# Attention feeding a two-layer MLP on one core: sums moved behind the landing of what they read, one pair turned on TensorE, and a wrapped batch turned in two DMA pieces

## The chip, the core and the metric

The kernel runs on one core of a Trainium2 chip. The metric is the device time of one execution in microseconds (us); lower is better. Time before: 416.68 us, the median of three runs (415.06, 416.68, 417.58).

## What is computed

```python
# q, k, v: (8, 12, 448, 64) f32;  moe_w_in: (768, 2048);  moe_w_out: (2048, 768)
scores = np.matmul(q, k.transpose(0, 1, 3, 2)) / np.sqrt(64)
attn = softmax(scores)                            # over the last axis
x = np.matmul(attn, v).transpose(0, 2, 1, 3).reshape(3584, 768)
h = x @ w_in
out = np.maximum(0.01 * h, h) @ w_out             # (3584, 768) f32
```

## The kernel before

**Units of work.** The heads of a batch are taken in twos: `NU` = 48 pairs, six (`HP`) to a batch. A pair is loaded from HBM by DMAs that GpSimd issues, cast to bf16 (`cast`, L168 and L170, mostly on GpSimd), and its q and k are turned so that the head's width lies on the partitions. Pairs below `NPE` = 14 are turned on TensorE (`transposes`, L253, copied out of PSUM by VectorE at L259), the others by a transposing DMA from SyncE's queue (`turn`, L236). A pair's scores are four chunks. Three chunks at a time are a **burst**: six matmuls (L270) into three PSUM slots, then three exponentials on ScalarE (L279). When a pair's four chunks are exponentiated, its **rows** follow: 32 matmuls of `e` with `v` (L750) into a slot, a reciprocal and a multiplication on VectorE (L756, L757) that write `x` and free the slot. Then `x` is turned into `xT`, the MLP's input with the model dimension on partitions: by a DMA on SyncE's queue, or for the pairs in `X_PE` (10 and 11 before) on TensorE (L318, copied by L319).

**The MLP** is done by regions of tokens, whose borders are `cuts` = 0, 640, 1152, 1664, 2176, 2688, 3072, 3584. Region 0 is done plainly: `head` takes its first 448 tokens (L352, ScalarE's activation L593), `neck` the other 192 (L616, activation L633, and `mix_h`, L430 and L431). Every later region is a two by two block product in seven products in place of eight, which needs sums of blocks: of w_in (`mix_w_in`, L385 and L389), of w_out (`mix_weights`, L364 to L371), of x (`mix_x_part`, L410) and of h. `hidden(i)` is the first layer of region i (L458), `second(i)` the second layer of region i (`block_pair`, L530; evicted and joined by VectorE at L535 and L538). In `second(i)` the rows of region i + 1 are finished, and its x sums are made there too, since `hidden(i + 1)` comes next.

**xT is a ring** of `NX` = 1920 tokens, with region 3 (token 1664) at place 0. Batch 3 (tokens 1344 to 1791) runs past the ring's end. Its rows are cut in chunks of 112 tokens, one of which straddles the end, 96 columns before it and 16 behind.

**Order.** All five engines run their instructions in the order in which the code emits them. Attention work is put between the matmuls of `head`, `neck` and `second` by `place`, a planner with a rough clock (`model`): it emits a burst, a turning on TensorE or a pair's rows when its model says that slots and inputs are free. SyncE's queue holds the transposing DMAs and the stores of the output in one order.

Of the kernel before, what the change touches and what calls it, by code (L numbers as in the profile page):

```python
# [10 lines left out]
BF16 = mybir.dt.bfloat16  # L11
# [5 lines left out]
def kernel(  # L17
# [9 lines left out]
    nc = tc.nc  # L27
# [3 lines left out]
    P = 128  # L31
# [63 lines left out]
    def place_of(t):  # L95
        return (t + NX - cuts[3]) % NX

    xT = xT_pool.tile([P, KD, NX], BF16)

    w_in_sb = w_pool.tile([P, KD, DF], BF16)  # L100
    w_out_sb = w_pool.tile([P, MD, DM], BF16)
# [133 lines left out]
    def turn(dst, src):  # L235
        nc.sync.dma_start_transpose(out=dst.rearrange("p (c s) -> p c s", s=SC), in_=src)  # L236
# [64 lines left out]
    def x_transposes(u, bank=None):  # L301
        b, hp = divmod(u, HP)
        at = place_of(b * S)
        if bank is None:
            x = x_t.pop(u).rearrange("p so h d -> p so (h d)")
            if at + S <= NX:
                turn(xT[:, hp, at:at + S], x.rearrange("p so n -> p (so n)"))
                return
            fit, rest = divmod(NX - at, SC)
            turn(xT[:, hp, at:at + fit * SC], x[:, :fit].rearrange("p so n -> p (so n)"))  # L310
            nc.sync.dma_start_transpose(out=xT[:, hp, NX - rest:], in_=x[:rest, fit])
            nc.sync.dma_start_transpose(out=xT[:, hp, :SC - rest], in_=x[rest:, fit])
            turn(xT[:, hp, SC - rest:at + S - NX], x[:, fit + 1:].rearrange("p so n -> p (so n)"))
            return
        dst = xT[:, hp, at:at + S]
        tr = turn_tile(bank)
        for so in range(NSC):
            nc.tensor.transpose(tr[:, 0, ts(so, SC)], x_t[u][:, so], ident[:SC, :SC])  # L318
        nc.vector.tensor_copy(dst, tr[:, 0, :])  # L319
# [37 lines left out]
    def mix_weights():  # L357

        pieces = [(slice(m, m + 2), slice(MH + m, MH + m + 2)) for m in range(0, MH, 2)]
        left, right = slice(0, NW), slice(NW, DM)  # L360
        for todo in (pieces[:2], pieces[2:]):
            for lo, hi in todo:
                t2, t3, t4 = (w_mix[:, x, lo] for x in range(3))
                nc.vector.tensor_sub(t3, w_out_sb[:, hi, right], w_out_sb[:, lo, right])  # L364
                yield
                nc.vector.tensor_add(t2, t3, w_out_sb[:, lo, left])
                yield
                nc.vector.tensor_sub(t4, w_out_sb[:, hi, left], t2)
                yield
            for lo, hi in todo:  # L370
                nc.vector.tensor_sub(w_out_sb[:, lo, right], w_out_sb[:, lo, right], w_out_sb[:, lo, left])  # L371
                yield

    def mix_w_in():
# [22 lines left out]
    def mix_x_part(i, ks):  # L397

        at = place_of(cuts[i])
        nh = (cuts[i + 1] - cuts[i]) // 2  # L400
        near, far = slice(ks.start, ks.stop), slice(KH + ks.start, KH + ks.stop)
        one, two = slice(at, at + nh), slice(at + nh, at + 2 * nh)
        t2, t3, t4 = (x_mix[:, x, near, :nh] for x in range(3))
        for o, x, y in (
            (t3, xT[:, far, two], xT[:, near, two]),
            (xT[:, near, two], xT[:, near, two], xT[:, near, one]),
            (t2, xT[:, far, two], xT[:, near, two]),
            (t4, xT[:, far, one], t2),
        ):
            nc.vector.tensor_sub(o, x, y)  # L410
            yield
# [172 lines left out]
    def head(ins, outs):  # L584

        for m in opened:
            part(0, m, (KD - 1,))
        for m in range(MD):
            if m not in opened:
                part(0, m, range(KH))  # L590
                yield KH * HEAD / 2400, False
                part(0, m, range(KH, KD))
            nc.scalar.activation(h[:, m, :HEAD], open_t.pop(m)[:, :HEAD], AX.Prelu, alpha=0.01)  # L593
            settle()
            if m == opened[-1]:
                slots.append(idle)
            if 5 <= m < 13:
                next(ins)
            if m >= 12:
                next(outs)  # L600
            yield (KH if m not in opened else 1) * HEAD / 2400, True

    def neck(outs):

        n = cuts[1] - HEAD
        at = place_of(HEAD)
        ms = [x + y for x in range(0, MH, 2) for y in (0, MH)]
        held = {}

        def part2(m, kks):  # L610
            fresh = m not in held
            if fresh:
                held[m] = next_bank()
            for j in range(2):
                for kk in kks:
                    nc.tensor.matmul(  # L616
                        held[m][:, j * n:(j + 1) * n], w_in_sb[:, kk, ts(m + j, P)], xT[:, kk, at:at + n],
                        start=(fresh and j == 0 and kk == 0), stop=(kk == KD - 1), skip_group_check=True,
                    )

        for m in ms[:2]:
            part2(m, range(KD - 1))
        yield 4 * (KD - 1) * n / 2400, False
        for x, m in enumerate(ms):
            if x < 2:
                assert rows_done >= need[1], rows_done
                settle_x()
                part2(m, (KD - 1,))
            else:
                part2(m, range(KH))  # L630
                yield 2 * KH * n / 2400, False
                part2(m, range(KH, KD))
            nc.scalar.activation(  # L633
                h[:, m:m + 2, HEAD:cuts[1]], held.pop(m)[:, :2 * n].rearrange("p (m t) -> p m t", m=2), AX.Prelu, alpha=0.01
            )
            settle()
            if m >= MH:
                mix_h(0, m - MH)
            for _ in range((1, 1, 1, 1, 0, 2, 2, 2)[x]):
                next(outs)  # L640
            yield 2 * (KH if x > 1 else 1) * n / 2400, True

# [136 lines left out]
            late.extend(todo[2:])  # L779
        chunk += len(todo)  # L780

    X_PE = (HP + 4, HP + 5)
    owed_x = []

    def settle_x(now=None):
# [42 lines left out]
    def place(i, want, soon=0, full=True, calm=True, first=False, lazy=False, keen=NU):  # L828
# [3 lines left out]
        while True:  # L832
# [14 lines left out]
            if want > done and state < 2 and turned(last) and not blocked and len(slots) == 3 and all(  # L847
# [13 lines left out]
                        ready[(start + x) // NSC] = model["act"] + 0.1  # L861
                model["now"] = now + 0.78
                continue
            u = rows_done
            if calm and whole and not (lazy and late) and at[0] <= now + 0.05 and ready.get(u, 0) <= now + 0.05 and (
                u <= (chunk + 5) // NSC - NE or u < keen
# [10 lines left out]
    def second(i):  # L877

        x_sums = [mix_x_part(i + 1, slice(0, 2)), mix_x_part(i + 1, slice(2, 3))] if i + 1 < NR else []
        fresh = [0, 0]  # L880
        left = plan[i]
        for c in range(len(spots(i)[1])):
            for x, _ in enumerate(block_pair(i, c)):
# [3 lines left out]
                    model["now"] += 0.65  # L887
                left -= place(i, left, calm=x not in (1, 3), keen=need[min(i + 2, NR)])
                if i == 0 and x % 2:
                    next(outs if c == 0 and x in (3, 5) else ins if x > 4 else iter(()), None)  # L890
                for y in range(2):
                    fresh[y] += i + 1 < NR and rows_done >= need[i + 2] - 1 + y and 14 * c + x > 4
                for y, todo in enumerate(x_sums):
                    if fresh[y] > 4 and next(todo, 0) is None:
                        break
        assert left == 0 or chunk == NU * NSC, (i, left)
        assert i + 1 == NR or rows_done >= need[i + 2], (i, rows_done)
# [62 lines left out]
```

## Time and profile before

| | |
|---|---|
| median of three runs | 416.68 us |
| the profiled execution | 413.6 us |
| its span | 411.8 us |
| TensorE busy | 385.3 us, 94% of the span |
| VectorE, ScalarE, GpSimd busy | 229.5, 264.8, 142.2 us |
| mean granted TensorE clock | 0.979 of full speed |

The profiled execution is 1.8 us longer than its span (launch and end lie outside), and 3.1 us below the median. A row of the timeline gives the start, the time to the end of the last of its instructions, the engine, the line, the operation, and in brackets how long the engine sat idle before it and what ended that. Matmuls overlap a little in the records, so the time from one row's start to the next row's start is the cost of a row.

### The profile page before, as it was taken

To read this page: it belongs to the slowest core of one execution; us is meant where nothing else is said; L and a number is where in the kernel's file an instruction comes from. 1 tells how busy PE (TensorE), PEld (TensorE's weight loads), DVE (VectorE), ACT (ScalarE), POOL (GpSimd) and SP (SyncE) were. 2 spreads that over 40 slices of the span, in tenths; PEclk is the share of its full clock that TensorE was granted. 3 is DMA by queue.
4 is the path that set the end of the run, shared out by engine and by line. 5 is a ranking of instruction groups with operands and counts; after the bars stand their busy time and mean duration, and the time that the engine had idled before them with its cause. 6 is when DMAs were issued, how large, how long until landed. Compare 5 with 4: busy or idle time off the path is not lost.

```text
span 411.8 us, 9991 instructions
## 1 busy us (share of the span) xinstructions
PE 385.3 (94%) x4074; PEld 263.2 (64%) x4074; DVE 229.5 (56%) x486; ACT 264.8 (64%) x391; POOL 142.2 (35%) x222
## 2 busy tenths in 40 slices
PE   8999976779979999599999999999999999999996
PEld 3564645555648855278655886558855597568854
DVE  3652543476665654354736656465665657384754
ACT  6987861565656877518777588774877668727800
POOL 8898722464346212334043620337112200000000
PEclk9999998699999999979999999999999999999999
DMA  9999999647978913759439891599818650222022
GB/s 137 198 202 203 177 176 194 86 65 113 181 110 141 161 33 61 154 100 170 69 84 152 132 169 26 105 153 167 112 24 149 87 123 2 60 63 78 2 66 88
DMA packets 95038, 47.09 MB, mean 114 GB/s; under 512 B 53648, under 2 KB 91664, under 8 KB 94992
## 3 DMA queue, kind: packets, MB, share of 16 engines
q0 software_dynamic: 38224, 22.58, 43.3%
q1 hardware_dynamic: 56704, 23.85, 28.9%
q8 instruction: 32, 0.52, 0.5%
q14 instruction: 14, 0.11, 0.1%
q10 hardware_dynamic: 64, 0.02, 0.0%
HBM read 45.61 MB, written 11.01 MB: 137 GB/s over the span
## 4 chain that ended last, share of the span: by engine, by line
PE 79%; DMA 8%; DVE 5%; SPq 3%; issue 2%; ACT 1%; POOL 1%; DVEq 0%; ACTq 0%; POOLq 0%
PE g L530 27%; PE g L458 13%; PE sc L458 13%; PE sc L750 9%; PE sc L270 7%; DMA xT<-x 6%; PE g L352 3%; PE g L616 2%; DMA w_in_mix<-in_k_dram 2%; PE g L289 2%; SPq L236 2%; PE g L253 1%; POOL w_in_mix L139 1%; DVE x L757 1%; DVE o L535 1%
## 5 line engine op out<-in xcount | busy, mean ns | idle before, releaser
L279 ACT ACTIVATE e<-sc 112x896 bf16<-112x896 f32 x192 | 163.1, 918 | 48.6 <-PE sc L270 48.3
L530 PEld LDWEIGHTS <-h 128*128 128x128 bf16 x680 | 62.0, 98 | 55.6 <-issue 22.4
L530 PE MATMUL g<-w_out_sb,h 128*128 128x384 bf16 x448 | 86.6, 330 | 7.3 <-DVE o L535 7.3
L168 POOL COPY qkb<-fq 112x512 bf16<-112x512 bf16 x38 | 26.9, 708 | 94.4 <-DMA qkT<-qkb 60.5
L447 ACT ACTIVATE h<-c 128x512 bf16<-128x512 f32 (+1 forms) x72 | 43.5, 611 | 24.0 <-DVE c L473 15.4
L458 PEld LDWEIGHTS <-w_in_sb 128*128 128x128 bf16 x576 | 54.7, 98 | 6.6 <-issue 0.7
L270 PE MATMUL sc<-qkT 64*128 64x448 bf16 x384 | 50.7, 356 | 7.3 <-DVE x L757 4.7
L750 PEld LDWEIGHTS <-e 112*128 112x128 bf16 x1344 | 48.1, 99 | 8.8 <-ACT e L279 6.5
L170 POOL COPY v<-fv 112x512 bf16<-112x512 bf16 x38 | 25.9, 684 | 74.7 <-PE sc L750 70.6
L750 PE MATMUL sc<-v,e 112*128 112x65 bf16 x1344 | 51.5, 196 | 0.0
L458 PEld LDWEIGHTS <-w_in_mix 128*128 128x128 bf16 x432 | 41.2, 98 | 4.1
L530 PE MATMUL g<-w_mix,h 128*128 128x384 bf16 (+1 forms) x224 | 41.9, 327 | 0.0
L270 PEld LDWEIGHTS <-qkT 64*128 64x128 bf16 x384 | 15.0, 94 | 34.6 <-issue 24.6
L535 DVE COPY o<-g 128x384 f32<-128x384 f32 x53 | 29.2, 552 | 13.0 <-PE g L530 12.5
L756 DVE RECIPROCAL rec<-sc 112x8 f32<-112x8 f32 x42 | 8.7, 207 | 44.2 <-PE sc L750 39.8
L168 POOL COPY qkb<-fk 112x512 bf16<-112x512 bf16 x38 | 24.6, 648 | 16.3 <-DMA fk<-in_k_dram 16.3
L757 DVE TENSOR_TENSOR x<-sc,rec 112x512 bf16<-112x512 f32 x42 | 29.0, 691 | 1.6 <-DVE rec L756 0.2
L538 DVE TENSOR_TENSOR o<-o,g 128x384 f32<-128x384 f32 x42 | 23.1, 550 | 10.7 <-PE g L530 10.7
L458 PE MATMUL g<-xT,w_in_sb 128*128 128x256 bf16 (+1 forms) x216 | 28.5, 268 | 0.3 <-DVE o L538 0.3
L458 PE MATMUL sc<-xT,w_in_sb 128*128 128x256 bf16 (+1 forms) x216 | 28.5, 268 | 0.0
L470 ACT COPY c<-g 128x512 f32<-128x512 f32 (+1 forms) x12 | 6.8, 569 | 31.6 <-PE g L458 26.6
L530 PE MATMUL g<-w_mix,hmix 128*128 128x384 bf16 x112 | 21.5, 327 | 0.0
(96 smaller groups left out, 471.8 us busy)
## 6 DMA issues: line engine op xcount, KB each, us to landing
fq<-in_q_dram POOLq DMA_DIRECT2D x19, 224.0 KB, 7.6
fk<-in_k_dram POOLq DMA_DIRECT2D x19, 224.0 KB, 9.1
fv<-in_v_dram POOLq DMA_DIRECT2D x19, 224.0 KB, 6.6
w_in_sb<-in_moe_w_in_dram POOLq DMA_DIRECT2D x4, 768.0 KB, 11.9
w_out_sb<-in_moe_w_out_dram POOLq DMA_DIRECT2D x4, 768.0 KB, 17.5
out_dram<-o SPq DMA_DIRECT2D x7, 336.0 KB, 3.5
out_dram<-o SPq DMA_DIRECT2D x8, 288.0 KB, 4.8
out_dram<-o SPq DMA_DIRECT2D x7, 240.0 KB, 3.1
```

The costliest lines, as they stand in the source:

```text
L168: by(qk_sb[u][:, x].rearrange("p so h d -> p h so d"), f)
L170: by(v_sb[u % NV][:, :, :, :D], f)
L270: nc.tensor.matmul(ps[:, j, :S], t[j * D:(j + 1) * D, S + c * SC:S + c * SC + P], t[j * D:(j + 1) * D, :S], start=True, stop=True,)
L279: nc.scalar.activation(e[:, :, c, :], sc_t.pop((u, c))[:SC, :, :S], AX.Exp, scale=scale)
L352: nc.tensor.matmul(open_t[m][:, :n], w_in_sb[:, kk, ts(m, P)], xT[:, kk, at:at + n], start=(fresh and kk == kks[0]), stop=(kk == KD - 1),)
L447: nc.scalar.activation(hs[:, m:m + 2, cols], x.rearrange("p (m t) -> p m t", m=2), AX.Prelu, alpha=0.01)
L458: nc.tensor.matmul(ps[:, j * nh:(j + 1) * nh], w[:, kk, ts(j, P)], x[:, kk], start=(first and j == 0 and kk == 0), stop=(kk == KH - 1), sk ...
L530: nc.tensor.matmul(ps[:, cols], x[:, m], w[:, m], start=(first and m == 0), stop=(m == MH - 1), skip_group_check=True,)
L535: by(o[:, at], ps[:, :NW])
L538: nc.vector.tensor_add(o[:, at], o[:, at], ps[:, :NW])
L750: nc.tensor.matmul(ps[:, j, qc, :], e[:, at:at + P], vt[:, j, c, :], start=(c == 0), stop=(c == NSC - 1),)
L757: nc.vector.tensor_mul(x_t[u].rearrange("p q j d -> p j q d"), ps[:SC, :, :, :D], rec.to_broadcast([SC, 2, NSC, D]))
```

## The change

1. **w_out sums behind their landing, w_in sums ahead.** In `head` the sums of w_in start at the fifth of sixteen steps and go on to the end; no w_out sum is left there. The sums of w_out start in `neck`, and the sum that writes the third block (`t4`) is made last of each half.
2. **Pair 9 turned on TensorE.** `X_PE` takes in pair 9. `place` may in `head` also turn a pair's q and k on TensorE ahead of the burst that needs them.
3. **Batch 3 in two pieces.** `xT` has 16 more columns. The straddling chunk is turned as one, so that its last 16 columns land in the first 16 of the next block; six small copies on VectorE bring them home before the sums of region 3.
4. **x sums later.** A region's x sums start when the model's clock has gone 7 us past the row that they wait for, in place of five steps of the loop.

```diff
+    OVER = SC - cuts[3] % S % SC
+    xT_flat = xT_pool.tile([P, KD * NX + OVER], BF16, name="xT")
+    xT = xT_flat[:, :KD * NX].rearrange("p (k t) -> p k t", k=KD)
...
-            fit, rest = divmod(NX - at, SC)
-            turn(xT[:, hp, at:at + fit * SC], x[:, :fit].rearrange("p so n -> p (so n)"))
-            nc.sync.dma_start_transpose(out=xT[:, hp, NX - rest:], in_=x[:rest, fit])
-            nc.sync.dma_start_transpose(out=xT[:, hp, :SC - rest], in_=x[rest:, fit])
-            turn(xT[:, hp, SC - rest:at + S - NX], x[:, fit + 1:].rearrange("p so n -> p (so n)"))
+            n = (NX + OVER - at) // SC
+            turn(xT_flat[:, hp * NX + at:(hp + 1) * NX + OVER], x[:, :n].rearrange("p so n -> p (so n)"))
+            turn(xT[:, hp, OVER:at + S - NX], x[:, n:].rearrange("p so n -> p (so n)"))
...   (mix_weights)
                 nc.vector.tensor_add(t2, t3, w_out_sb[:, lo, left])
                 yield
-                nc.vector.tensor_sub(t4, w_out_sb[:, hi, left], t2)
+            for lo, hi in todo:
+                nc.vector.tensor_sub(w_out_sb[:, lo, right], w_out_sb[:, lo, right], w_out_sb[:, lo, left])
                 yield
             for lo, hi in todo:
-                nc.vector.tensor_sub(w_out_sb[:, lo, right], w_out_sb[:, lo, right], w_out_sb[:, lo, left])
+                nc.vector.tensor_sub(w_mix[:, 2, lo], w_out_sb[:, hi, left], w_mix[:, 0, lo])
...   (mix_x_part)
+        if at == 0:
+            for hp in range(KD - 1) if ks.start == 0 else (KD - 1,):
+                nc.vector.tensor_copy(xT[:, hp, :OVER], xT_flat[:, (hp + 1) * NX:(hp + 1) * NX + OVER])
+            yield
...   (head)
-            if 5 <= m < 13:
+            if m >= 4:
                 next(ins)
-            if m >= 12:
-                next(outs)
...   (neck)
-            for _ in range((1, 1, 1, 1, 0, 2, 2, 2)[x]):
+            for _ in range((1, 1, 1, 1, 1, 1, 1, 3)[x]):
                 next(outs)
...
-    X_PE = (HP + 4, HP + 5)
+    X_PE = (HP + 3, HP + 4, HP + 5)
...   (place, behind the burst)
+            u = to["pe"]
+            if first and full and state == 0 and u < min(NPE, to["cast"] - 1) and u - NQ < chunk // NSC and model["act"] <= now + 0.6:
+                transposes(u)
+                to["pe"] += 1
+                state = 1
+                model["now"] += 0.45
+                continue
...   (second)
-        fresh = [0, 0]
+        fresh = [None, None]
...
-                    next(outs if c == 0 and x in (3, 5) else ins if x > 4 else iter(()), None)
+                    next(outs if c == 0 and x < 12 else ins, None)
                 for y in range(2):
-                    fresh[y] += i + 1 < NR and rows_done >= need[i + 2] - 1 + y and 14 * c + x > 4
+                    if fresh[y] is None and i + 1 < NR and rows_done >= need[i + 2] - 1 + y:
+                        fresh[y] = model["now"] + 7.0
                 for y, todo in enumerate(x_sums):
-                    if fresh[y] > 4 and next(todo, 0) is None:
+                    if fresh[y] is not None and fresh[y] <= model["now"] and next(todo, 0) is None:
                         break
```

Line numbers of the changed program are a few higher than before: its L386 is L385 of before, L415 is L410, L540 is L535, L543 is L538, L760 and L761 are L756 and L757, L238 is L236.

On VectorE, late in `head` and before, around the rows of pair 9 (`w_mix` takes w_out sums, `w_in_mix` w_in sums, `rec` and `x` belong to rows):

```order
L364 TENSOR_TENSOR w_mix<-w_out_sb 128x768
L756 RECIPROCAL rec_1024<-sc_105 112x8
L757 TENSOR_TENSOR x<-sc_105,rec_1024 112x2x4x64
L366 TENSOR_TENSOR w_mix<-w_mix,w_out_sb 128x768
L368 TENSOR_TENSOR w_mix<-w_out_sb,w_mix 128x768
```

The same place of the changed program, with the turned x of pair 9 copied at L319:

```order
L386 TENSOR_TENSOR w_in_mix<-w_in_sb,w_in_mix 128x3x256
L760 RECIPROCAL rec_1019<-sc_105 112x8
L761 TENSOR_TENSOR x<-sc_105,rec_1019 112x2x4x64
L386 TENSOR_TENSOR w_in_mix<-w_in_sb,w_in_mix 128x3x256
L261 COPY qkT_114<-g_102 128x896
L319 COPY xT<-sc_104 128x448
```

The w_out sum that stood ahead of the row's reciprocal is gone from here, and the copy of a turned q and k (`qkT`) has come in from `neck`.

On SyncE's queue, in `second(1)`, from the stores to the last row of batch 3, before:

```order
L331 DMA out_dram<-o 16x768
L236 DMA_TRANSPOSE qkT_116<-qkb 128x8x112
L236 DMA_TRANSPOSE qkT_117<-qkb 128x8x112
L236 DMA_TRANSPOSE xT<-x 128x2x112
L311 DMA_TRANSPOSE xT<-x 128x96
L312 DMA_TRANSPOSE xT<-x 128x16
L236 DMA_TRANSPOSE xT<-x 128x1x112
L236 DMA_TRANSPOSE xT<-x 128x2x112
```

And in the changed program:

```order
L331 DMA out_dram<-o 16x768
L238 DMA_TRANSPOSE qkT_116<-qkb 128x8x112
L238 DMA_TRANSPOSE qkT_117<-qkb 128x8x112
L238 DMA_TRANSPOSE xT<-x 128x3x112
L238 DMA_TRANSPOSE xT<-x 128x1x112
L238 DMA_TRANSPOSE xT<-x 128x3x112
L238 DMA_TRANSPOSE xT<-x 128x1x112
L238 DMA_TRANSPOSE qkT_114<-qkb 128x8x112
```

Each of the six pairs of batch 3 has two entries there in place of four.

On VectorE, in the second block pair of `second(1)`, around the first x sum, before:

```order
L535 COPY o<-g_102 128x384
L410 TENSOR_TENSOR x_mix<-xT 128x512
L410 TENSOR_TENSOR xT<-xT 128x2x256
L535 COPY o<-g_103 128x384
L410 TENSOR_TENSOR x_mix<-xT 128x512
```

And in the changed program:

```order
L540 COPY o<-g_102 128x384
L540 COPY o<-g_103 128x384
L415 TENSOR_TENSOR x_mix<-xT 128x512
L543 TENSOR_TENSOR o<-o,g_102 128x384
L415 TENSOR_TENSOR xT<-xT 128x2x256
```

The first x sum stands behind the eviction of bank `g_103` where it stood ahead of it.

More of the change, by code (lines that the diff above doesn't have):

```diff
@@ L96, in place_of @@
         return (t + NX - cuts[3]) % NX
-    xT = xT_pool.tile([P, KD, NX], BF16)
+    OVER = SC - cuts[3] % S % SC
+    xT_flat = xT_pool.tile([P, KD * NX + OVER], BF16, name="xT")
+    xT = xT_flat[:, :KD * NX].rearrange("p (k t) -> p k t", k=KD)
     w_in_sb = w_pool.tile([P, KD, DF], BF16)
@@ L362, in mix_weights @@
             for lo, hi in todo:
-                t2, t3, t4 = (w_mix[:, x, lo] for x in range(3))
+                t2, t3 = w_mix[:, 0, lo], w_mix[:, 1, lo]
                 nc.vector.tensor_sub(t3, w_out_sb[:, hi, right], w_out_sb[:, lo, right])
@@ L619, in part2 @@
                     )
+        assert all(u == need[1] - 1 for u, _ in owed_x), owed_x
         for m in ms[:2]:
```

## The prediction

> **What bounds the kernel now.** First the page: who is busy, and in which of 40 slices (10.3 us each) TensorE is not.
>
> ```profile
> PE 385.3 (94%) x4074; PEld 263.2 (64%) x4074; DVE 229.5 (56%) x486; ACT 264.8 (64%) x391; POOL 142.2 (35%) x222
> PE   8999976779979999599999999999999999999996
> PEclk9999998699999999979999999999999999999999
> ```
>
> TensorE is the bound: busy 94%, the next engine 64%. Its holes lie in the sixth to ninth slice (51 to 93 us), the twelfth and the seventeenth, and the granted clock drops with the first and the last of them. What time there is to win is idle and slow TensorE in these places. Then TensorE's two largest waits (us in all, times, longest):
>
> ```profile
> PE g L530 <- DVE o L535: 7.3, 4, 4.2
> PE sc L270 <- DVE x L757: 4.7, 2, 2.8
> ```
>
> Both are put down to short VectorE work, so I looked in the timeline at what stood ahead of it. In the neck:
>
> ```profile
> 57.94 0.56 DVE L364 TENSOR_TENSOR w_mix<-w_out_sb 128x768 bf16<-128x768 bf16 x1 [4.88 <-DMA w_out_sb<-in_moe_w_out_dram]
> 58.65 0.69 DVE L757 TENSOR_TENSOR x<-sc,rec 112x512 bf16<-112x512 f32 x1
> 59.40 0.36 PE L270 MATMUL sc<-qkT 64*128 64x448 bf16 x2 [1.90 <-DVE x L757]
> 59.37 1.73 SPq L236 DMA_TRANSPOSE xT<-x  x1
> 68.20 1.56 PE L616 MATMUL g<-xT,w_in_sb 128*128 128x192 bf16 x17 [2.02 <-DMA xT<-x]
> 92.72 0.36 PE L270 MATMUL sc<-qkT 64*128 64x448 bf16 x2 [2.80 <-DVE x L757]
> ```
>
> A w_out sum waits 4.88 us for its weights and holds up the x of pair 9 behind it, which holds a slot that the burst at 56.95 needs (1.90), and whose transposing DMA starts only at 59.37 and lands 8.8 us later (2.02). At the borders of regions it is an x sum that stands ahead of an eviction:
>
> ```profile
> 119.56 0.81 PE L530 MATMUL g<-w_out_sb,h 128*128 128x384 bf16 x4 [2.39 <-DVE o L535]
> 169.94 0.36 PE L270 MATMUL sc<-qkT 64*128 64x448 bf16 x2 [0.81 <-DMA qkT<-qkb]
> 173.06 0.42 DVE L410 TENSOR_TENSOR x_mix<-xT 128x512 bf16<-128x512 bf16 x1 [6.93 <-DMA xT<-x]
> 174.46 1.44 PE L530 MATMUL g<-w_out_sb,h 128*128 128x384 bf16 x4 [4.16 <-DVE o L535]
> 226.78 0.81 PE L530 MATMUL g<-w_out_sb,h 128*128 128x384 bf16 x4 [0.35 <-DVE o L535]
> 325.96 0.81 PE L530 MATMUL g<-w_out_sb,h 128*128 128x384 bf16 x4 [0.37 <-DVE o L535]
> ```
>
> **The neck, priced as a stretch.** From the burst at 56.95 to the third product at 94.33 TensorE needs 37.38 us. What would the same matmuls cost undisturbed? These rows of the chain give the price of each kind:
>
> ```profile
> 36.51 0.68 PE sc L270 x6
> 37.18 1.24 PE g L352 x6
> 82.83 1.04 PE sc L750 x32
> 81.24 1.59 PE g L616 x18
> 93.09 2.06 PE g L530 x12
> ```
>
> The stretch holds 5 bursts (3.4), 12 matmuls of L352 (2.5), 4 rows (4.2), 96 of L616 (8.5), 16 of L530 (2.7), and four small turnings on TensorE, some 0.3 us each (1.2): 22.5 us. So **14.9 us are lost**, more than the waits alone, since the clock drops:
>
> ```profile
> 59.40:62.80 3.40, 3.40 (x39) 2.46 (x39) 1.18 (x2) 1.35 (x2) 2.98 (x4) 0.67 1.24 211
> 76.00:79.50 3.50, 3.50 (x25) 3.33 (x23) 1.69 (x4) 0.55 (x2) 2.28 (x4) 0.50 0.16 32
> 119.50:123.60 4.10, 3.79 (x48) 2.58 (x48) 3.87 (x12) 0.00 (x0) 1.42 (x2) 1.00 0.51 56
> 174.40:177.60 3.20, 3.14 (x37) 2.46 (x37) 1.23 (x4) 0.00 (x0) 0.62 (x1) 0.50 1.05 122
> ```
>
> (The number ahead of the last two is the granted clock.) What the change takes from these 14.9 us: the sum ahead of pair 9's x is gone, and with it the 1.90; w_out is first touched in the neck, behind the 57.94 at which its first parts had landed. Pair 9 turned on TensorE removes the 2.02 and costs four matmuls (0.3) and a VectorE copy. Pairs 12 and 13, which the neck turned between waits for ScalarE and VectorE, are now turned in the head, behind casts that were done early, the last at 51.8 us:
>
> ```profile
> 51.16 0.62 POOL L168 COPY qkb<-fk 112x512 bf16<-112x512 bf16 x1
> ```
>
> So the waits that go are those that lowered the clock.
>
> What stays, followed by hand through the new order with these durations:
>
> ```profile
> 85.24 1.73 ACT L279 ACTIVATE e<-sc 112x896 bf16<-112x896 f32 x2 [0.36 <-PE sc L270]
> 86.85 0.49 ACT L633 ACTIVATE h<-g 128x384 bf16<-128x384 f32 x1
> 85.89 0.96 DVE L364 TENSOR_TENSOR w_mix<-w_out_sb 128x768 bf16<-128x768 bf16 x1
> ```
>
> - Between two bursts of the neck ScalarE has three exponentials (2.6) and some three activations (0.4 from start to start): 3.8 us against 3.5 of TensorE work. With the two exponentials ahead of the activation that frees a bank, TensorE waits about 1.3 us.
> - Pair 11's rows now follow their burst at once, ahead of the last exponential: 0.7.
> - Pair 9's turning stands between its x and the next burst: 0.6.
> - All sixteen w_out sums now lie in the neck and the product behind it, and each takes 0.55 to 0.96 us. In front of the last two rows VectorE is again late: the h sums wait for ScalarE's activation, and the row's reciprocal stands behind them and the w sums. I get 1.8 us at the burst before the last activation and 2.1 at the burst where it was 2.80.
>
> Together 6.5 us, and 0.3 for the new turning: the neck gains 14.9 - 6.8 = **8.1 us**. Both ends: nothing of the four remains (14.6), or they are twice as long, 13 us, and nearly nothing is gained (1.6).
>
> Here the Trainium skill, "TensorE: Matmul & The Clock Gate", section "Part 1: The HAM clock gate", speaks: the clock halves after an idle window of about 3.4 us, and the window runs freely. By that rule waits of 1.8 and 2.1 us cost no clock and the sum stays as it is. The trace is harsher at one place: after 1.90 us without work the clock was granted at 0.67 for 3.4 us, while after 2.39 us it stayed at 1.00. By the harsher row each of the two waits would cost 1.1 us more (3.4 x 0.33), and the sum would be 2.2 smaller.
>
> **The borders.** Border 1 (`second(0)`, 119.56): the first x sum moves behind the joins of the fifth and sixth product.
>
> ```profile
> 107.70 2.05 PE sc L750 x64
> 117.03 0.80 DVE L410 TENSOR_TENSOR x_mix<-xT 128x512 bf16<-128x512 bf16 x1 [3.31 <-DMA xT<-x]
> ```
>
> Its data landed at 117.0, 7.3 us after these matmuls. In the new order the sixth product ends 7.2 us behind them and its join some 0.9 later, so the sum finds them there. Behind it wait only a row's x and the last eviction, and the next layer's first two products use other banks. **2.4 us** gained; a landing later by 1.5 us would still be hidden, one later by 4 gives nothing.
>
> Border 2 (`second(1)`, 174.46) is priced as a stretch too.
>
> ```profile
> 168.50:180.74 12.24, 7.28 (x56) 4.26 (x56) 4.36 (x12) 2.88 (x4) 4.85 (x8) 0.72 0.61 87
> 161.10 0.69 DVE L757 TENSOR_TENSOR x<-sc,rec 112x512 bf16<-112x512 f32 x1
> 169.37 1.19 SPq L236 DMA_TRANSPOSE xT<-x  x1
> 178.25 1.82 SPq L236 DMA_TRANSPOSE xT<-x  x1
> ```
>
> A burst (0.7), 16 matmuls of L530 (2.7) and a row (1.0) take 4.4 us undisturbed: 7.8 are lost, to the 0.81, the 4.16 and the halved clock behind them. SyncE's queue is the cause: a piece takes 1.2 us there however small, a row of batch 3 has four, and the x that is ready at 161.8 is first served at 169.37, the last piece of the next row at 178.25. With two pieces the two rows ahead of it save some 5 us and its own 2.5: pair 22 lands at about 168, pair 23 at 171. The first x sum now stands behind the fourth product's eviction, about 168, pair 23's behind the sixth's join, not before 171.7. All **7.8 us** go; if the queue gains no more than its own pieces, half of the 4.16 stays with its clock: 3 gained.
>
> Borders 3 and 5 give their 0.35 and 0.37: **0.7**. Border 4 gets six copies of 16 columns on VectorE. No row shows one: nothing below, and above the 0.29 of a sum of 256 columns (next row), 1.7 in all. I take a cost of nothing, since the fifth product (8 matmuls, 1.4) runs beside them on a free bank; without that cover 1.7.
>
> Border 6 could lose: its sums start behind the sixth join, not the third copy.
>
> ```profile
> 370.59 0.29 DVE L410 TENSOR_TENSOR x_mix<-xT,x_mix 128x256 bf16<-128x256 bf16 x1
> 373.52 0.82 PE L458 MATMUL g<-x_mix,w_in_mix 128*128 128x256 bf16 x6
> ```
>
> The last sum, now done at 370.9, comes about 3 us later, and the product at 373.52 reads sums that are done at 372 to 373.7: **0.2** lost, 1 at most.
>
> **Sum.** 8.1 + 2.4 + 7.8 + 0.7 - 0.2 = 18.8 us, against the profiled execution's 413.6: 394.8. That execution lies 3.1 us below the median of the runs, 416.7, and the same sum against the median gives 397.9. The profiled run is as good a sample as the three, and the waits that go are of a kind that differs from run to run (DMA landings, the clock's phase), so I forecast between them, **396 us**; its own range is 391 to 400, the two references with 3 us about.
>
> **Rivals.**
>
> - *The neck holds back half.* VectorE is late as before, because the sixteen w sums came to it in place of the one that waited; a wait of 2 to 3 us at each of three bursts lowers the clock again. For it: the 2.80 at 92.72 is this mechanism already, and the sums of 0.96. Against: the neck's waits before were mostly others. It keeps 4 to 6 us more: 400 to 404.
> - *Everything goes.* ScalarE and VectorE keep up, since the planner gives fewer bursts to the neck than my hand order makes them wait for. 14.6 in place of 8.1: 387 to 391.
> - *The x sums wait on.* The change would not do what it says at the borders if landings came as late as the sums: SyncE's queue runs behind TensorE by its own length and moves with it. For it: 6.93 us of waiting at 173.06. Against: six pairs with two entries less. Borders 1 and 2 then give 4 in place of 10: 402 to 405.
> - *Slower: the supply doesn't follow.* Pairs from 14 on come through load, cast, transposing DMA, and these have their own times.
>
> ```profile
> 72.97 0.62 POOL L168 COPY qkb<-fq 112x512 bf16<-112x512 bf16 x1 [7.91 <-DMA qkT<-qkb]
> ```
>
>   Pair 15's cast waits until pair 14's DMA has landed, 72.9; the new order asks for pair 14 at about 75.6. If TensorE runs into the supply there, it may wait at each of the eight bursts of `second(0)` too. The kernel is slower than before from the point at which such a wait, with the halved clock behind it, costs 2.6 us on the mean (8 x 2.6 = 20.7, all that the forecast gains); at 3 us it gives 420. Against: in the trace TensorE waits for a turned pair once, 0.81 us, and that in the congestion that goes.
>
> **How the numbers follow.** Chances: the forecast 0.60, half held back 0.16, everything 0.11, sums wait on 0.08, slower 0.05. From 390 to 404 hold the forecast, nearly all of half held back and a part of the others, some 0.8. A measurement of this kernel tells no change from about 1%, 4.2 us: faster than 412.5 holds for all but the last case and a few per cent of mishaps between. Faster 0.92, same 0.04, slower 0.04.
>
> **What would show it.** Right: no w_out sum waits for its DMA; no matmul of L616 waits for `xT<-x`; the first product's start in the region of 78 us in place of 87.97; one or two waits of some 2 us left between 70 and 85 us, on VectorE's x; the third product near 86; no wait over 0.5 us at a border; SyncE's entries for batch 3 twelve, each 1.2 us; granted clock 1.00 in every stretch from the neck on. Wrong: a clock under 0.8 in the neck, turnings in the head waiting for GpSimd's casts, x sums waiting several us, or bursts of `second(0)` waiting for `qkT<-qkb`.

## The result, and the profile after

The changed kernel takes **401.68 us** (median of four runs, 400.43 to 402.49) against 415.87 us (four runs) of the kernel before: a ratio of 0.9653, 95% interval 0.9604 to 0.9702. That is 14.2 us faster. The profiled execution takes 400.97 us (its span 399.2), 12.6 less than the one before, where the prediction's sum had 18.8. The medians below are over all executions, while the ratios leave out four that took longer at a lower granted clock (one of e4, two of e11, and the one of e9 that was profiled).

The page of the changed kernel, TensorE's busy share and its granted clock in 40 slices (now 10.0 us each):

```profile
PE 380.3 (95%) x4078; PEld 259.8 (65%) x4078; DVE 232.8 (58%) x493; ACT 264.5 (66%) x391; POOL 143.6 (36%) x222
PE   7999999869999999999996999979999999999996
PEclk9999999999999999999996999999999999999999
```

The holes of the twelfth and the seventeenth slice are gone and those of the neck are fewer (the eighth and ninth slice). But two new ones have come, in the 22nd and the 27th, and the clock drops with the first of them. TensorE's largest waits (us in all, times, longest) name them:

```profile
PE g L463 <- DVE o L543: 5.7, 2, 3.2
PE sc L272 <- DVE x L761: 4.5, 2, 3.2
```

In the first row the first layer of a region (L463) waits for the join behind the sixth product (L543); before, such waits came to 0.3 us in all. How long each region takes is read from one start of a first layer to the next, with the regions' borders as windows (us, then busy us of TensorE, its weight loads, VectorE, ScalarE, GpSimd, the granted clock, DMA share and GB/s). Before, from the first layer of region 1 to that of region 4:

```profile
123.63:180.74 57.11, 52.15 (x521) 35.72 (x521) 28.85 (x60) 35.50 (x52) 19.06 (x30) 0.94 0.72 106
180.74:230.41 49.67, 49.32 (x522) 34.45 (x521) 29.66 (x59) 35.50 (x52) 16.36 (x26) 1.00 0.80 121
230.41:279.89 49.48, 49.48 (x521) 34.29 (x520) 29.22 (x59) 35.51 (x52) 17.06 (x27) 1.00 0.79 117
```

The same stretches of the changed kernel:

```profile
110.91:160.41 49.50, 49.50 (x521) 34.29 (x520) 30.95 (x62) 35.36 (x52) 19.69 (x31) 1.00 0.91 125
160.41:213.23 52.82, 49.62 (x522) 34.37 (x521) 30.47 (x63) 35.43 (x52) 19.74 (x33) 0.99 0.78 116
213.23:267.96 54.73, 52.23 (x521) 35.94 (x521) 29.34 (x61) 35.63 (x52) 16.05 (x27) 0.95 0.63 106
```

The first layer of region 1 starts 12.7 us earlier (110.91 for 123.63), border 2 gives 7.6 more, and then the stretches up to borders 3 and 4 take 3.2 and 5.3 back. Without these 8.4 us the profiled execution would lie at 392.6.

The neck of the changed kernel, in the timeline of TensorE (its last two waits, the first and the third product):

```profile
75.32 0.36 PE L272 MATMUL sc<-qkT 64*128 64x448 bf16 x2 [1.28 <-DVE x L761]
76.61 1.46 PE L535 MATMUL g<-w_out_sb,h 128*128 128x384 bf16 x8
84.07 0.37 PE L272 MATMUL sc<-qkT 64*128 64x448 bf16 x2 [3.19 <-DVE x L761]
84.37 1.48 PE L535 MATMUL g<-w_mix,h 128*128 128x384 bf16 x8
```

Border 3 in the timelines of VectorE, SyncE's queue and TensorE:

```profile
206.76 0.42 DVE L415 TENSOR_TENSOR x_mix<-xT 128x512 bf16<-128x512 bf16 x1
208.47 0.69 DVE L761 TENSOR_TENSOR x<-sc,rec 112x512 bf16<-112x512 f32 x1
209.18 1.73 SPq L238 DMA_TRANSPOSE xT<-x  x1
212.08 0.63 DVE L415 TENSOR_TENSOR xT<-xT 128x512 bf16<-128x512 bf16 x1 [2.92 <-DMA xT<-x]
212.64 0.54 DVE L543 TENSOR_TENSOR o<-o,g 128x384 f32<-128x384 f32 x1
213.23 1.44 PE L463 MATMUL g<-xT,w_in_sb 128*128 128x256 bf16 x6 [3.16 <-DVE o L543]
```

And border 4:

```profile
263.86 0.69 DVE L761 TENSOR_TENSOR x<-sc,rec 112x512 bf16<-112x512 f32 x1
264.57 1.20 SPq L238 DMA_TRANSPOSE xT<-x  x1
267.00 0.44 DVE L415 TENSOR_TENSOR x_mix<-xT 128x512 bf16<-128x512 bf16 x1 [2.45 <-DMA xT<-x]
267.36 0.54 DVE L543 TENSOR_TENSOR o<-o,g 128x384 f32<-128x384 f32 x1
267.96 0.81 PE L463 MATMUL g<-xT,w_in_sb 128*128 128x256 bf16 x6 [2.50 <-DVE o L543]
```

What is odd: the row at 208.47 is pair 30, the first pair of the *next* batch. Its DMA writes columns 576 to 1023 of xT's first block. The sum at 212.08 belongs to region 3 and touches columns 0 to 511 of the first two blocks. It had its data: the sum at 206.76 had read half of the same columns 5 us before. At border 4 it is pair 36 (columns 1024 to 1471) and a sum that reads 768 to 1023. Each of the two idle times ends when just that DMA lands, 2.9 us behind its entry at 209.18 and 2.4 behind the one at 264.57. The sum doesn't use what it brings; the join, and with it TensorE, wait behind the sum.

### The profile page after: what moved, and what is told of

It reads as the page before. It is cut to its first block, busy times and chain, and to the rows that moved or that the text cites. A ratio compares the mean times of both kernels' runs of the same rounds, so it can differ in the third digit from the quotient of the medians.

```text
span 399.2 us, 9983 instructions
## 1 busy us (share of the span) xinstructions
PE 380.3 (95%) x4078; PEld 259.8 (65%) x4078; DVE 232.8 (58%) x493; ACT 264.5 (66%) x391; POOL 143.6 (36%) x222
## 4 chain that ended last, share of the span: by engine, by line
PE 87%; DVE 4%; DMA 3%; ACT 2%; issue 1%; POOL 1%; DVEq 0%; POOLq 0%; ACTq 0%
PE g L535 31%; PE g L463 14%; PE sc L463 13%; PE sc L754 11%; PE sc L272 9%; PE g L352 4%; DMA w_in_mix<-in_k_dram 2%; PE g L291 2%; ACT e L281 1%; DMA xT<-x 1%; PE g L619 1%; PE g L255 1%; DVE x L761 1%; POOL w_in_mix L141 1%; PE sc L352 1%
## 5 line engine op out<-in xcount | busy, mean ns | idle before, releaser
L535 PEld LDWEIGHTS <-h 128*128 128x128 bf16 x680 | 61.2, 98 | 47.3 <-issue 13.7
L535 PE MATMUL g<-w_out_sb,h 128*128 128x384 bf16 x448 | 85.2, 326 | 0.0
L463 PEld LDWEIGHTS <-w_in_sb 128*128 128x128 bf16 x576 | 55.5, 99 | 13.1 <-issue 6.3
L170 POOL COPY qkb<-fq 112x512 bf16<-112x512 bf16 x38 | 25.6, 674 | 78.1 <-DMA qkT<-qkb 47.2
L754 PEld LDWEIGHTS <-e 112*128 112x128 bf16 x1344 | 47.0, 99 | 9.6 <-ACT e L281 8.0
L172 POOL COPY v<-fv 112x512 bf16<-112x512 bf16 x38 | 25.1, 663 | 73.0 <-PE sc L754 66.8
L754 PE MATMUL sc<-v,e 112*128 112x65 bf16 x1344 | 50.7, 195 | 0.3 <-ACT e L281 0.3
L463 PEld LDWEIGHTS <-w_in_mix 128*128 128x128 bf16 x432 | 41.2, 98 | 4.1
L535 PE MATMUL g<-w_mix,h 128*128 128x384 bf16 (+1 forms) x224 | 41.4, 324 | 0.0
L540 DVE COPY o<-g 128x384 f32<-128x384 f32 x53 | 29.3, 552 | 19.5 <-PE g L535 18.9
L760 DVE RECIPROCAL rec<-sc 112x8 f32<-112x8 f32 x42 | 8.7, 206 | 45.7 <-PE sc L754 45.5
L170 POOL COPY qkb<-fk 112x512 bf16<-112x512 bf16 x38 | 27.7, 730 | 20.7 <-DMA fk<-in_k_dram 20.6
L463 PE MATMUL g<-xT,w_in_sb 128*128 128x256 bf16 (+1 forms) x216 | 29.8, 276 | 5.7 <-DVE o L543 5.7
L543 DVE TENSOR_TENSOR o<-o,g 128x384 f32<-128x384 f32 x42 | 23.1, 550 | 14.7 <-PE g L535 14.6
L761 DVE TENSOR_TENSOR x<-sc,rec 112x512 bf16<-112x512 f32 x42 | 29.0, 691 | 1.6 <-DVE rec L760 0.2
L463 PE MATMUL sc<-xT,w_in_sb 128*128 128x256 bf16 (+1 forms) x216 | 29.3, 273 | 0.0
L535 PE MATMUL g<-w_mix,hmix 128*128 128x384 bf16 x112 | 21.5, 326 | 0.0
```

The costliest lines, as they stand in the source:

```text
L170: by(qk_sb[u][:, x].rearrange("p so h d -> p h so d"), f)
L172: by(v_sb[u % NV][:, :, :, :D], f)
L463: nc.tensor.matmul(ps[:, j * nh:(j + 1) * nh], w[:, kk, ts(j, P)], x[:, kk], start=(first and j == 0 and kk == 0), stop=(kk == KH - 1), sk ...
L535: nc.tensor.matmul(ps[:, cols], x[:, m], w[:, m], start=(first and m == 0), stop=(m == MH - 1), skip_group_check=True,)
L540: by(o[:, at], ps[:, :NW])
L543: nc.vector.tensor_add(o[:, at], o[:, at], ps[:, :NW])
```

## The experiments

Each is timed against the kernel before on its own chip.

| run | us | before | ratio, 95% interval |
|---|---|---|---|
| e1: changed, x sums by block | 394.30 | 414.51 | 0.9512 (0.9468 to 0.9556) |
| e2: changed, x sums at their old time | 395.81 | 414.51 | 0.9562 (0.9507 to 0.9617) |
| e3: before, two pieces alone | 406.46 | 414.51 | 0.9817 (0.9769 to 0.9866) |
| e4: before, the neck's parts alone | 401.99 | 414.51 | 0.9683 (0.9627 to 0.9739) |
| e5: before, w sums alone | 412.50 | 414.68 | 0.9956 (0.9929 to 0.9983) |
| e6: before, pair 9 alone | 411.31 | 414.68 | 0.9921 (0.9888 to 0.9954) |
| e7: before, early turning alone | 407.35 | 414.68 | 0.9831 (0.9795 to 0.9867) |
| e8: e1, w_out sums spread | 392.58 | 414.68 | 0.9473 (0.9438 to 0.9508) |
| e9: changed, xT in blocks | 395.49 | 413.52 | 0.9537 (0.9499 to 0.9575) |
| e10: before, later x sums alone | 410.17 | 413.52 | 0.9904 (0.9868 to 0.9940) |
| e11: e8, w_out sums spread otherwise | 391.66 | 413.52 | 0.9447 (0.9418 to 0.9476) |

**e1, the x sums by block.** The edit in `mix_x_part`:

```diff
-            nc.vector.tensor_sub(o, x, y)
+            if o is t4:
+                nc.vector.tensor_sub(o, x, y)
+            else:
+                for k in range(ks.stop - ks.start):
+                    nc.vector.tensor_sub(o[:, k], x[:, k], y[:, k])
```

> The changed kernel with the x sums of a region's first two blocks of columns written as one instruction for each block (three more on VectorE a region), in the same order. Theory A, a wait for the wrong transfer: in the changed kernel one x sum of border 3 waits 2.92 us and one of border 4 waits 2.45 us on VectorE for the transposing DMA of a row of the NEXT batch, which stands just ahead of it and whose columns the sum does not read; the join of the sixth product stands behind it (TensorE 3.16 and 2.50 us, then 6.3 us at a granted clock of 0.54). An instruction that spans two blocks is taken by the dependency tracking to touch that row, one that stays in a block is not. Then both waits go and the stretches from one hidden layer to the next go from 52.82 and 54.73 us back to 49.5: 8.6 us less, 393 us. Theory B, landings as such are late at these places (SyncE's queue): the sums wait on for their own pairs, 399 to 402. Theory C, VectorE is full there (copies, sums): three more instructions make it worse, 402 to 403.

394.30 us, near theory A's 393; theory B had 399 or more. Border 3 of this run, where the row of pair 30 (207.92) still stands ahead of the second sum:

```profile
207.92 0.69 DVE L765 TENSOR_TENSOR x<-sc,rec 112x512 bf16<-112x512 f32 x1
208.53 0.48 DVE L419 TENSOR_TENSOR xT<-xT 128x256 bf16<-128x256 bf16 x2
208.93 0.55 DVE L547 TENSOR_TENSOR o<-o,g 128x384 f32<-128x384 f32 x1
209.53 0.81 PE L467 MATMUL g<-xT,w_in_sb 128*128 128x256 bf16 x6
```

The sum follows the row at once, the join follows the sum, and TensorE doesn't wait. The more instructions are no burden, so theory C falls. Against its own kernel before, e1 gains 20.2 us where the changed kernel gains 14.2.

**e9, the tile in blocks again.** The order of the changed kernel and its sums over two blocks stay; the tile has three dimensions as before, and pair 23 alone is turned in four pieces. (The 16 columns of pair 22 are then overwritten by pair 23, so the output of this kernel is not right; its instructions and transfers are the ones described.)

```diff
-    xT_flat = xT_pool.tile([P, KD * NX + OVER], BF16, name="xT")
-    xT = xT_flat[:, :KD * NX].rearrange("p (k t) -> p k t", k=KD)
+    xT = xT_pool.tile([P, KD, NX], BF16)
+    xT_flat = xT.rearrange("p k t -> p (k t)")
...
+            if hp == KD - 1:
...
-            for hp in range(KD - 1) if ks.start == 0 else (KD - 1,):
+            for hp in range(KD - 1) if ks.start == 0 else ():
```

> The changed kernel, order and x sums (of two blocks at once) as changed, but with the tile of the turned x declared as six blocks of 1920 columns again in place of one flat row with 16 columns more; only the last pair of batch 3, which needs those 16, is turned in four pieces (two entries of 1.2 us more on SyncE). Theory A, sharpened: the dependency tracking knows the blocks of a tile with three dimensions and makes a sum wait only for a row that it reads; on the flat row it takes a sum over two blocks to touch what lies between. Then the waits of borders 3 and 4 go with the order unchanged: 393 to 395 us, as with sums by block. Theory B, the sums' new place behind a row of the next batch is late whatever the tile: 401 to 402.

395.49 us, near theory A's 393 to 395; theory B had 401 to 402. With the same sums in the same places the loss is gone when the tile is declared in blocks. From its profile only the order of events at border 3 is read: the same sum over two blocks runs right behind pair 30's x, before that row's DMA has even started on SyncE's queue, and no x sum of the run waits for a DMA.

```profile
244.79 0.69 DVE L768 TENSOR_TENSOR x<-sc,rec 112x512 bf16<-112x512 f32 x1
245.40 0.41 DVE L422 TENSOR_TENSOR xT<-xT 128x512 bf16<-128x512 bf16 x1
245.51 1.19 SPq L238 DMA_TRANSPOSE xT<-x  x1
```

So the wait came from the *declaration*: on the flat row the program can make a sum that spans two blocks wait for a DMA into columns between them. It doesn't always. At borders 1 and 5 of the changed kernel a row of the next batch also stands ahead of such sums (the second and third at border 1, the third at border 5), its DMA writes between their pieces, and they did not wait. Why not isn't settled.

**e2, the x sums at their old time**, on the flat tile:

```diff
-        fresh = [None, None]
+        fresh = [0, 0]
...
-                    if fresh[y] is None and i + 1 < NR and rows_done >= need[i + 2] - 1 + y:
-                        fresh[y] = model["now"] + 7.0
+                    fresh[y] += i + 1 < NR and rows_done >= need[i + 2] - 1 + y and 14 * c + x > 4
...
-                    if fresh[y] is not None and fresh[y] <= model["now"] and next(todo, 0) is None:
+                    if fresh[y] > 4 and next(todo, 0) is None:
```

> The changed kernel with the rule of before for when the x sums start (a count of steps behind the rows, no delay of 7 us); all else as changed. Theory A (the sums' new place behind the next batch's row is what costs borders 3 and 4): these two give back 8.6 less their old 0.35 each, border 1 gets its 2.39 again, border 2 keeps most of its gain since SyncE has two pieces in place of four: 396 to 400 us. Rival: the later sums, not the shorter queue, carried the gain at border 2; then its 7.8 comes back too and the time is 403 to 405.

395.81 us, just below theory A's range. The sums stand ahead of the next batch's row again, and borders 3 and 4 cost nothing. Border 1 pays for it: an x sum waits 3.23 us for its own pair at 107.97, and TensorE 1.85. Border 2 stays good, so the later sums did not carry the gain there. Against its own kernel before, e2 gains 18.7 us and the changed kernel 14.2, so in the changed kernel the later sums cost some 4.5 us on balance (their two intervals overlap a little). Without their false wait they gain 1.5 us on e2 (e1), which lies within the intervals: by the times alone it isn't shown that they are worth having.

**e3, two pieces alone.** Of the change's diff the parts on `xT_flat`, `x_transposes` and `mix_x_part`; its core:

```diff
+            turn(xT_flat[:, hp * NX + at:(hp + 1) * NX + OVER], x[:, :n].rearrange("p so n -> p (so n)"))
+            turn(xT[:, hp, OVER:at + S - NX], x[:, n:].rearrange("p so n -> p (so n)"))
```

> The kernel before with batch 3 turned in two pieces alone (with its six copies), nothing else. By the prediction's border 2 (an entry takes 1.2 us on SyncE, two of four go for each row) pair 22 lands some 4 us earlier against the work, and the 4.16 us wait with the half clock behind it goes mostly: 408 to 410 us. Rival: SyncE's queue runs behind TensorE and moves with it, the sum stands as far ahead as before and the wait stays: 414 to 416.

406.46 us, 8.05 less than before, and 1.5 below the 408 to 410 that was expected. Its region from border 1 to border 2:

```profile
127.64:177.42 49.78, 49.32 (x522) 34.45 (x520) 28.52 (x58) 35.50 (x52) 18.03 (x28) 1.00 0.76 118
```

7.3 us less than the 57.11 of before, without any later sum: SyncE's queue was the cause.

**e10, the later sums alone** (tile in blocks, four pieces):

```diff
-        fresh = [0, 0]
+        fresh = [None, None]
...
-                    fresh[y] += i + 1 < NR and rows_done >= need[i + 2] - 1 + y and 14 * c + x > 4
+                    if fresh[y] is None and i + 1 < NR and rows_done >= need[i + 2] - 1 + y:
+                        fresh[y] = model["now"] + 7.0
...
-                    if fresh[y] > 4 and next(todo, 0) is None:
+                    if fresh[y] is not None and fresh[y] <= model["now"] and next(todo, 0) is None:
```

> The kernel before with the later x sums alone (7 us behind their rows), the tile in blocks, batch 3 in four pieces. Theory A: no wait of borders 3 and 4 arises, since the tile is in blocks; border 1 gives its 2.39, borders 3 and 5 their 0.7, border 2 between nothing and its 7.8 (the prediction gave the gain there to queue and order together; two pieces alone have taken all of it): 404 to 411.5. Rival: the later place as such costs 8.6 at borders 3 and 4: 412 to 420.

410.17 us, 3.35 less, within theory A's range. Borders 3 and 4 are clean (one wait of 0.29 us). At border 2 the queue of four pieces shows what remains, the wait moved from one place to the next:

```profile
177.69 0.29 DVE L410 TENSOR_TENSOR x_mix<-xT 128x256 bf16<-128x256 bf16 x1 [3.73 <-DMA xT<-x]
178.50 0.81 PE L458 MATMUL g<-xT,w_in_sb 128*128 128x256 bf16 x6 [2.38 <-DVE o L535]
```

**e4 to e7, the neck and its three parts.** e4 has the three edits of the neck, without those of xT and of the x sums; e5, e6 and e7 have one each. The lines that stand for them:

```diff
+            for _ in range((1, 1, 1, 1, 1, 1, 1, 3)[x]):
...
+    X_PE = (HP + 3, HP + 4, HP + 5)
...
+            if first and full and state == 0 and u < min(NPE, to["cast"] - 1) and u - NQ < chunk // NSC and model["act"] <= now + 0.6:
```

> The kernel before with the neck's parts alone: order and place of the w_out and w_in sums, pair 9 turned on TensorE, pairs 12 and 13 turned in the head; batch 3 still in four pieces and x sums at their old time. The prediction's term is 8.1 us, the changed kernel's trace shows 10.0 by the third product of the first region: 406 to 408 us, with the waits of borders 1 and 2 (2.39, 4.16) in place. Rival: the neck gains only with the shorter queue of SyncE behind it: 411 or more.

> The kernel before with the order and place of the w_out and w_in sums alone (pair 9 still turned by a DMA, pairs 12 and 13 turned where they were). Theory A, the neck's parts add up by the prediction's waits: the 1.90 us in front of the burst goes with the 3.4 us at a clock of 0.67 behind it (1.1), and pair 9's transposing DMA starts some 2 us earlier, so that most of the 2.02 goes too; the sums now stand in the neck and cost part of it again: 3 to 5 us less, 409.5 to 411.5. Rival B, the sum that waited for its weights (4.88 us) started the whole chain of the neck, clock included: 7 us or more, 407 or less. Rival C: the sums only move the load to where VectorE is late already: 414 or more.

> The kernel before with the rows of pair 9 turned on TensorE, nothing else. Theory A: the 2.02 us in front of the neck's matmuls goes, 0.3 us of turning come, the 1.90 stays: 1 to 2 us less, 412.5 to 413.5. Rival B, the chain starts elsewhere: no change, 414 to 415.

> The kernel before with pairs turned on TensorE in the head as soon as their casts are done, nothing else. Theory A: the waits of 0.48, 0.58 and 0.79 us around the two turnings in the neck go, and the 3.5 us at a clock of 0.50 behind them (1.75): 2 to 3.6 us less, 411 to 412.5. Rival B: the same four matmuls come in the head and the neck waits for ScalarE's activation (1.60 us) and VectorE's x (2.80) as before: 414 to 415.

The whole neck gives 12.5 us, the parts 2.2, 3.4 and 7.3. None of the four came out in its theory's range: e4 and e7 gained more than any theory gave them, e6 more than its theory A, and e5 less than its theory A. From the first matmul of `head` to the third product TensorE needs 68.4 us before, 66.9 in e5, 65.0 in e6, **57.6 in e7**, 58.1 in e4 and 58.7 in the changed kernel. In this stretch the edit of e7 alone does all of it. In e5 and e6, with one wait gone, the other grew in its place:

```profile
66.44 2.80 PE L615 MATMUL g<-xT,w_in_sb 128*128 128x192 bf16 x17 [2.97 <-DMA xT<-x]
```

```profile
59.84 0.37 PE L318 MATMUL sc<-ident,x 112*128 112x112 bf16 x4 [2.60 <-DVE x L758]
```

(The first is e5: pair 9's DMA, 2.97 for 2.02. The second is e6: its x behind the w_out sum, 2.60 for 1.90.) In e7 a wait of 1.81 stands there too, but no turning follows it, and the clock is granted at 1.00 over the whole neck. But e7's edit does more than move turnings: `place` then puts pair 9's rows ahead of the first w_out sum, which stood ahead of them before.

```profile
55.49 0.69 DVE L757 TENSOR_TENSOR x<-sc,rec 112x512 bf16<-112x512 f32 x1
57.20 0.56 DVE L364 TENSOR_TENSOR w_mix<-w_out_sb 128x768 bf16<-128x768 bf16 x1 [0.56 <-DMA w_out_sb<-in_moe_w_out_dram]
```

The sum waits 0.56 us in place of 4.88, and the 1.90 in front of a burst is gone. So e7 takes out this link as well as the turnings of the neck, and no run separates the two.

e7 keeps 7.3 of these 10.8 us, because border 1 comes sooner and its x doesn't:

```profile
110.65 0.75 DVE L410 TENSOR_TENSOR x_mix<-xT 128x512 bf16<-128x512 bf16 x1 [5.33 <-DMA xT<-x]
```

```profile
113.14 1.44 PE L530 MATMUL g<-w_mix,h 128*128 128x384 bf16 x4 [3.28 <-DVE o L538]
```

```profile
104.00:117.41 13.41, 9.23 (x74) 5.23 (x73) 5.36 (x12) 6.64 (x8) 6.01 (x10) 0.76 1.09 187
```

In this stretch, up to the first layer of region 1, the clock is granted at 0.76. With all three parts (e4) TensorE waits 0.89 there, and the way from the third product to the first layer of region 1 takes 29.1 us against 32.8 in e7. That is 3.7 of the 5.2 us between the two runs; so the other two parts earn most of their share at border 1.

**e8 and e11, a better version.** On e1, the neck hands out its w_out sums otherwise (the edit of e8; e11 has 3, 2, 2, 2, 1, 0, 2, 0 there):

```diff
-            for _ in range((1, 1, 1, 1, 1, 1, 1, 3)[x]):
+            for _ in range((1, 2, 2, 2, 2, 0, 3, 0)[x]):
...
-                if i == 0 and x % 2:
+                if i == 0 and x % 2 and (c or x > 4):
```

> The changed kernel with the x sums written by block (as in the run with that change) and the w_out sums of the neck handed out as 1, 2, 2, 2, 2, 0, 3, 0 behind its eight groups in place of 1, 1, 1, 1, 1, 1, 1, 3, and none in the first product behind it. Theory A: the two waits left in the neck (1.17 and 1.53 us there) are those sums standing ahead of a row's reciprocal; in their new places VectorE waits for ScalarE anyway. Both waits go, 2.7 us less than that run's 394.3: 391 to 392.5. Rival B: GpSimd's casts, beside which a sum of 128x768 takes 0.96 us in place of 0.55, or ScalarE's activations are what is late there: 394.

> The kernel with x sums by block and the neck's w_out sums handed out as 3, 2, 2, 2, 1, 0, 2, 0 (1, 2, 2, 2, 2, 0, 3, 0 in the run that moved them first). VectorE is idle for some 3 us at 64 to 67 there, and its sums at 71 to 73, beside GpSimd's casts, took 0.7 to 0.96 us in place of 0.55. Theory A: the 1.75 us that TensorE still waits at 75.5 is this work; it shrinks to 0.5 to 1.4: 391.2 to 392.3 us. Rival B: the h sum behind ScalarE's activation (done at 73.8) is what holds the row: no change, 392.6. Rival C: the first w_out parts land later than the sums now want them: 393 or more.

392.58 and 391.66 us, both faster than the changed kernel by more than their intervals. Against e1 the intervals overlap, so it isn't shown that handing out the sums otherwise gains anything on top of the sums by block. Of the two waits of e1 (1.17 and 1.53 us) the second is gone in e8, as theory A on e8 had it; the first has grown, which it had not:

```profile
75.49 0.37 PE L272 MATMUL sc<-qkT 64*128 64x448 bf16 x2 [1.75 <-DVE x L765]
82.18 0.74 PE L272 MATMUL sc<-qkT 64*128 64x448 bf16 x6
```

Behind the 1.75 the clock was granted at 0.59 for 4.2 us, which eats what the second wait gave: the neck takes 27.4 us in e8 and 26.9 in e1. Between e8 and e11 the intervals overlap too; which of them is better stays open, and so which of the three theories on e11 holds.

## Why the prediction was right or wrong

401.68 us lies above the forecast's own range of 391 to 400, and inside the 390 to 404 that was given over all cases. That it came so near is partly luck: the places where gains were forecast gave more than the 18.8 us of the sum, and a loss that stood in no term took 8.4 off again.

- **The neck, 8.1.** Measured 8.8 (37.38 us before; 55.75 to 84.37, 28.62 us, now), and 1.2 more in the head, where the burst starts at 55.75 in place of 56.95. What stays was priced at 6.8 and measured at 6.1; the waits at 1.3, 0.7, 1.8 and 2.1 came out as 0.64, 0.34, 1.28 and 3.19, and none of them lowered the clock here, as the harsher row would have had it. (In e4, with the same neck, a wait of 2.30 at the last place did.) The 3.19 is of one execution: in e1 and e2, with the same neck, this wait is 1.53, and the stretch takes 26.9 and 27.3 us. The size held. The order of the *reasons* did not: the waiting w_out sum and pair 9's DMA, named first, are worth 2.2 and 3.4 by themselves, with the other wait grown in the place of the one that went. The early turning, named last, gives the most, 7.3; but e7 also takes out the 1.90 behind the waiting w_out sum, so how much is due to the turnings that left the neck stays open.
- **Border 1, 2.4.** 29.30 us became 26.54: 2.8. e10 has 27.1 there with later sums alone, and e2, without them, 29.6.
- **Border 2, 7.8.** 7.6, by the cause that was named, SyncE's entries of 1.2 us (e3). That the order of the x sums was needed too was wrong (e2).
- **Borders 3 and 5, 0.7, and the six copies, nothing: the step that failed.** Border 3 lost 3.2 us, and the half clock behind it 2.8; border 4 lost 2.5; border 5 gave 0.3. The prediction asked what stands *behind* a later x sum only at border 1, and never which row now stands *ahead* of it, and it read the new declaration of xT as 16 columns more. The sums then waited for the DMA of the next batch's row ahead of them, whose columns they don't read (e1, e9). It also put the copies at border 4; they stand at border 3, where five take 1.74 us and nobody waits.
- **Border 6, -0.2.** 40.90 us became 40.52 from there to the end of the span; no wait.

Of the rivals "the x sums wait on" was nearest: sums waiting for DMAs, and 402 us. But it was meant for borders 1 and 2 and for data that is late. Neither happened. ("The neck holds back half" had 400 to 404, but the neck held nothing back.) Of the signs named, those of the neck were seen, the first product at 76.61 and the third at 84.37; "no wait over 0.5 us at a border" and a clock of 1.00 from the neck on were not. With the measured terms and the failed step left out, the sum is 12.7 (to the first layer of region 1) + 7.6 + 0.7 (border 5 and the end) = 21.0, and e1, the kernel without that step's fault, gives 20.2.

## What to carry to other kernels

When work is moved to a later place, list what now stands ahead of it on its own engine as well as behind it, and each DMA that it has been moved past, also those whose data it doesn't read. A tile's declaration is part of the schedule: views of a flat tile can wait for transfers into columns between their pieces (here at two borders of the four where one lay there), and cutting an instruction at the blocks, or the tile into blocks, takes such a wait away. The row of a wait is not its price. Undo one link of a chain at a time, and look whether the next wait grows in its place; look also at what else the planner moved, or two links are undone as one.

## What the runs showed of the hardware

The length of a wait alone doesn't tell whether the clock drops. After the 3.16 us at 213.23 it did, and stayed low for 6.3 us; after the 2.50 us at 267.96 it didn't, nor after the 3.19 us at 84.07. (After 1.75 us in e8 and 2.30 in e4 it did, at 0.59 and 0.54.) The rows of the changed kernel:

```profile
213.20:219.50 6.30, 6.27 (x56) 4.96 (x56) 3.66 (x11) 1.17 (x2) 2.30 (x4) 0.54 1.09 205
268.00:276.00 8.00, 8.00 (x97) 7.26 (x97) 4.64 (x12) 4.39 (x9) 4.61 (x7) 1.00 1.06 143
84.37:110.91 26.54, 26.54 (x301) 15.44 (x299) 17.69 (x35) 18.65 (x22) 15.24 (x22) 1.00 0.92 147
```

The Trainium skill, "TensorE: Matmul & The Clock Gate", section "Part 1: The HAM clock gate", has the gate look at windows that run freely, which agrees with equal waits that end differently; its idle window of about 3.4 us is longer than the 3.16 here, the 1.90 of before and the 1.75 of e8, which were all followed by a lower clock.

A w_out sum of 128x768 takes 0.55 us on VectorE by itself and up to 0.96 beside GpSimd's casts, and the casts 0.62 and up to 0.94 (e8):

```profile
67.92 0.55 DVE L364 TENSOR_TENSOR w_mix<-w_out_sb 128x768 bf16<-128x768 bf16 x1
72.13 0.96 DVE L364 TENSOR_TENSOR w_mix<-w_out_sb 128x768 bf16<-128x768 bf16 x1
72.63 0.94 POOL L172 COPY v<-fv 112x512 bf16<-112x512 bf16 x1
```

That they slow each other is read from their lying side by side; it wasn't tried by itself. But it fits the 3.19 us of the neck against the 1.53 of e1. In the changed kernel's profile three w_out sums ahead of that x lie beside casts and take 0.96, 0.85 and 0.96 us; in e1, with the same order in the neck, GpSimd ran no cast between 79.4 and 81.8, and the three take 0.55, 0.56 and 0.55. With the h sum behind them (1.09 for 0.68) that is 1.5 of the 1.7 us:

```profile
78.98 0.96 DVE L364 TENSOR_TENSOR w_mix<-w_out_sb 128x768 bf16<-128x768 bf16 x1
79.47 0.94 POOL L170 COPY qkb<-fq 112x512 bf16<-112x512 bf16 x1
79.75 0.55 DVE L364 TENSOR_TENSOR w_mix<-w_out_sb 128x768 bf16<-128x768 bf16 x1
83.32 0.36 PE L272 MATMUL sc<-qkT 64*128 64x448 bf16 x2 [1.53 <-DVE x L765]
```

(The first two rows are of the changed kernel, the others of e1.)
